# Gate products on VectorE, quartered group loads and a later first stage in a fused FFT and MLP kernel with gradients (one Trainium2 core)

## The chip, the cores and the metric

The kernel runs on one NeuronCore of one Trainium2 chip. A core has five engines that run their own instruction queues: TensorE (PE in the profile, with its weight loads as PEld), VectorE (DVE), ScalarE (ACT), GpSimd (POOL) and SyncE (SP). In this kernel SP issues the loads and POOL issues the stores and a few small loads. The metric is the device time of one launch in microseconds, as the median of several runs.

## The reference, cut to what matters

The reference runs a forward function and its gradients for eight inputs. S is 2048, D is 1024, F is 3584, and all data is bf16.

```python
g = sigmoid((x * gate_w).sum(-1, keepdims=True))
a = irfft2(rfft2(x) * (w_r + 1j * w_i))           # over S and D
h = relu(x @ w1 + b1);  b = (h * h) @ w2 + b2
out = g * a + (1 - g) * b
# B_x is not used in either branch; the outputs are out and the gradients
# of A_x, A_w_r, A_w_i, B_w1, B_b1, B_w2, B_b2, gate_w
```

Both branches and the gate read the same x, A_x in the call. The gate needs one dot product of 1024 elements for each of the 2048 rows.

## The kernel before, in words

The rows of x and of the incoming gradient are cut into 16 tiles of 128 rows (NT = 16). The kernel is written in a language in which tiles come from pools with a tag and a number of buffers. The waits between engines are derived from what each instruction reads and writes, and the order of each engine's queue is planned at build time, from the order of the code (as a priority) and from when inputs are thought to be ready. `after(ins, earlier)` (L210) adds a dependency by hand: a real wait, or, with `NoSync`, only an order. The order of the work is otherwise set by Python generators: each `yield` ends a step, and `spread` (L948) takes a given number of steps of a side generator for every step of a main one.

**MLP in (L635).** `mlp_in` makes the hidden layer and its gradient, transposed. `hidden` (L644) is eight matmuls of 512 columns into a PSUM tile `ph` (L647); ACT writes `rT` (L649) and its square `h2T` (L650). `grads` (L653) is eight matmuls into `pd` (L657), and DVE writes `dhT` (L661). `ph` and `pd` share one tag with two buffers. Both need transposed inputs: `xT` from x, and `dbT` from `dbn`, the incoming gradient scaled by 1 - g. `turn_tile` (L571) makes these with eight TensorE transposes of 128 columns into a PSUM tile `pt`, copied out by ACT for x (`turn_x`) and by DVE for the gradient (`turn_grad`). `pt`, the gate's `pg` and other small PSUM tiles share a tag `tr` with two buffers.

**The gate (L584).** For a group of four row tiles, `gate` runs 32 matmuls with one output column each (L590): a block of xT is the stationary operand and a column of `gwcol` (gate_w turned into columns by `vectors`, L578) the moving one. ACT makes the two sigmoids `omg` = 1 - g and `gcol` = g (L594, L595), and DVE scales four tiles of dbn in place by omg (L597).

**The start (L976 to L1029).** Seven matmuls on zeros warm TensorE up. Then, by hand: four tiles of x are loaded, turned and gated, and a loop over k = 0 to 3 interleaves eight units of `mlp_in` (four hidden, four grads) with the turning of four gradient tiles, and with the loads, turning and gating of the next four x tiles. The first stage of the FFT of x (`first_stage_of_x`, L599, with `folds` on DVE, `row_stage` L244 and `first_columns` L256 on TensorE) starts at the end of k = 0. After the loop 72 further units are mixed with the rest of this stage and with the same stage of the gradient, 0.9 steps a unit (L1036).

**Weight gradients and the middle of the FFT (L743, L415, L473).** `mlp_grads` runs 14 jobs: seven groups of 512 hidden columns of h2 against dbn (L786, gradient of w2) and seven of dh against x (L802, gradient of w1). A job is eight units of 16 matmuls of 512 columns; after each unit ACT copies the result to `wo` (L790, L807), and POOL stores it. The operand `grp` of a job is a group of h2 or dh that is read back from DRAM and turned by the DMA (`group`, L749, through `turned`, L166): four loads of 512 KB, in a tile with two buffers. They are written at the start of the job before the one that uses them. `spread` (L1054) mixes `fft_mid` and half of `fft_out` into the jobs, so that the SP queue also carries their loads z, w, amat, apmat and r. In `fft_out`, `folded` (DVE, L495) and `rows_back` (L503) use a loaded tile r, `columns_back` (L282 by `column_stage`) gives `pui`, ACT copies it to `e` (L512, L513), DVE makes `yo` (L529), and POOL stores it to `ax_scr` (L532).

**MLP out (L827).** The last stage makes the output (L872) and the gradient of x (L932), with the rest of `fft_out`. The change doesn't touch it. The multiply-and-sum operation that the change uses for the gate is already used there (L850, on f32 and bf16).

Of the kernel before, what the change touches and what calls it, by code (L numbers as in the profile page):

```python
# [10 lines left out]
P = 128  # L11
# [114 lines left out]
def kernel(  # L126
# [63 lines left out]
    kf = pers.tile([P, P], FDT, name="kf", tag="kf")  # L190
    cols = lambda n, w, dt=FP32: pers.tile([P] + w, dt, name=n, tag=n)
    gcol, omg, gpg, aGo, dsc = (cols(n, [NT]) for n in ("gcol", "omg", "gpg", "aGo", "dsc"))
    gwcol = cols("gwcol", [DC], BF16)
    bGo = cols("bGo", [NT, NH])
    gb1part = cols("gb1part", [FC, g.NSB])
    b1col = cols("b1col", [FC])
# [276 lines left out]
    def fft_out():  # L473
# [62 lines left out]
                    ld(out=w2[:, fc : fc + 4, :], in_=B_w2[fc * P : (fc + 4) * P, :].rearrange("(q p) e -> p q e", p=P))  # L536

        load(0), load(1)
        folded(0)
        for n in range(len(tiles) + 1):  # L540
            if n < len(tiles):
                rows_back(n)
                yield
            if n > 0:
                columns_back(n - 1)
            if n + 2 < len(tiles):
                load(n + 2)
            if n + 1 < len(tiles):
                folded(n + 1)
            yield  # L550
# [24 lines left out]
            nc.tensor.transpose(pt[:, b, :], src[:, b * P : (b + 1) * P], identb[:])  # L575
        copy(out=dst[:, :, of_tile(i)], in_=pt[:])

    def vectors(vrow):  # L578
        vps = tps.tile([P, FC + DC], BF16, name="vps", tag="tr", bufs=2)
        nc.tensor.transpose(vps[:], vrow[:], identb[: FC + DC, : FC + DC])  # L580
        nc.vector.tensor_copy(out=b1col[:], in_=vps[:, 0:FC])
        nc.vector.tensor_copy(out=gwcol[:], in_=vps[:, FC : FC + DC])

    def gate(i0):  # L584

        c_ = slice(i0, i0 + 4)
        pg = tps.tile([P, 4], FP32, name="pg", tag="tr", bufs=2)
        for i in range(i0, i0 + 4):
            for dc in range(DC):
                mm(  # L590
                    pg[:, i - i0 : i - i0 + 1], lhsT=xT[:, dc, of_tile(i)], rhs=gwcol[:, dc : dc + 1],
                    start=(dc == 0), stop=(dc == DC - 1), skip_group_check=True,
                )
        nc.scalar.activation(omg[:, c_], pg[:], ACT.Sigmoid, scale=-1.0)  # L594
        nc.scalar.activation(gcol[:, c_], pg[:], ACT.Sigmoid)  # L595
        for i in range(i0, i0 + 4):
            nc.vector.tensor_scalar(out=dbn[:, i, :], in0=dbn[:, i, :], scalar1=omg[:, i : i + 1], scalar2=None, op0=ALU.mult)  # L597

# [144 lines left out]
    def mlp_grads():  # L743
# [2 lines left out]
        strm = later["strm"]  # L746
        acc = wb.tile([P, D], FP32, name="dbacc", tag="dbacc")

        def group(scr, fg, earlier=None):  # L749
            t_ = strm.tile([P, NT, FGW], BF16, name="grp", tag="strm", bufs=2)  # L750
            v_ = scr[:].rearrange("c p s -> (c p) s")[fg * FGW : (fg + 1) * FGW, :]
            for k in range(4):
                after(turned(t_[:, 4 * k : 4 * (k + 1), :], v_[:, 4 * k * P : 4 * (k + 1) * P]), earlier)
            return t_

        xr = []
        jobs = [(h2T_scr, fg) for fg in range(FG)] + [(dhT_scr, fg) for fg in range(FG)]
        nxt = group(*jobs[0], later["blocks"])
        nc.vector.tensor_copy(out=acc[:], in_=dbn[:, 0, :])
        for t in range(1, NT):  # L760
            V(out=acc[:], in0=acc[:], in1=dbn[:, t, :], op=ALU.add)
        for n, (scr, fg) in enumerate(jobs):
            cur = nxt
            if n + 1 == len(jobs):
                later["block"] = blocks(h2T_scr)(0)
            else:
                nxt = group(*jobs[n + 1], later["blocks"])
            if n == 1:
                column_sums(wb, tps, "tr", acc, out_7)

# [9 lines left out]
            if scr is h2T_scr:  # L780
                for fb_ in range(FGC):
                    wo = wb.tile([P, D], BF16, name="wo2", tag="wo2", bufs=2)
                    for hf in range(NH):
                        pw = mps.tile([P, H], FP32, name="pw", tag="pw", bufs=2)
                        for t in range(NT):
                            mm(  # L786
                                pw[:], lhsT=cur[:, t, fb_ * P : (fb_ + 1) * P], rhs=dbn[:, t, hf * H : (hf + 1) * H],
                                start=(t == 0), stop=(t == NT - 1),
                            )
                        last = nc.scalar.copy(out=wo[:, hf * H : (hf + 1) * H], in_=pw[:])  # L790
                        if n in (2, 3):
                            x_ = wb.tile([P, D], BF16, name=f"res1_{len(xr)}", tag=f"res1_{len(xr)}")
                            after(ld(out=x_[:], in_=x_perm[len(xr)]), last)
                            xr.append(x_)
                        yield 3
                    f0 = fg * FGW + fb_ * P
                    st(out=out_6[f0 : f0 + P, :], in_=wo[:])
            else:
                for d_ in range(DC):
                    pw = mps.tile([P, FGW], FP32, name="pw", tag="pw", bufs=2)  # L800
                    for t in range(NT):
                        mm(  # L802
                            pw[:], lhsT=xr[t][:, d_ * P : (d_ + 1) * P], rhs=cur[:, t, :],
                            start=(t == 0), stop=(t == NT - 1),
                        )
                    wo = wb.tile([P, FGW], BF16, name="wo1", tag="wo1", bufs=3)
                    nc.scalar.copy(out=wo[:], in_=pw[:])  # L807
                    st(out=out_4[d_ * P : (d_ + 1) * P, fg * FGW : (fg + 1) * FGW], in_=wo[:])
                    yield 3
        mpss.close()  # L810
# [162 lines left out]
        turn_tile(dbT, i, dbn[:, i, :], nc.vector.tensor_copy)  # L973


    zeros = f1.tile([P, H], BF16, name="zeros", tag="zeros")  # L976
    nc.vector.memset(zeros[:], 0.0)
    pz = tps.tile([P, H], FP32, name="pz", tag="tr", bufs=2)
    for _ in range(7):
        mm(pz[:], lhsT=zeros[:, 0:P], rhs=zeros[:], start=True, stop=True)  # L980

    units = mlp_in()
    rows_of_x(0)
    vrow = f1.tile([FC + DC, P], BF16, name="vrow", tag="vrow")
    st(out=vrow[0:FC, :], in_=B_b1.rearrange("(fc p) -> fc p", p=P))
    st(out=vrow[FC : FC + DC, :], in_=gate_w.rearrange("(fc p) -> fc p", p=P))
    next(units)
    rows_of_grad(0)
    st(out=kf[:], in_=cten["kf"].ap())
    for i in range(4):  # L990
        turn_x(i)
    vectors(vrow)
    gate(0)
    next(units)
    rows_of_x(1)
# [2 lines left out]
    for k in range(NT // 4):  # L998
# [1 line left out]
        if k + 1 < NT // 4:  # L1000
            rows_of_grad(k + 1)
        next(units)
        turn_grad(i), turn_grad(i + 1)
        next(units)
        turn_grad(i + 2)
        next(units)
        turn_grad(i + 3)
        next(units)
        if stage:
            next(stage)  # L1010
        next(units)
        if k + 1 < NT // 4:
            turn_x(i + 4), turn_x(i + 5)
        next(units)
        if k + 1 < NT // 4:
            turn_x(i + 6), turn_x(i + 7)
        next(units)
        if k + 1 < NT // 4:
            gate(4 * (k + 1))
        if k + 2 < NT // 4:  # L1020
            rows_of_x(k + 2)
        if k == 0:
            for n in range(3):
                xs[n] = source(n, x_perm)
            stage = first_stage_of_x()
        next(stage)
        next(units)
        next(stage)
    V(out=gpg[:], in0=gcol[:], in1=omg[:], op=ALU.mult)  # L1029
    def firsts():  # L1030
        yield from stage
# [1 line left out]

    first = firsts()
    n = 0
    mixed = spread(units, first, 0.9)  # L1036
    while n < 72:
        next(mixed)
        n += 1
# [10 lines left out]

    spec, grads = spectra(), mlp_grads()
    next(grads), next(grads)
    todo = 1 + 12 * (S2 // 2) + 2 * NT
    for _ in spread(grads, spec, todo / (2.0 * FG * FGC * NH - 2)):  # L1054
        pass
    tps_s.close()
# [38 lines left out]
```

## Time and profile before

| | |
|---|---|
| time, median of 3 runs | 1309.12 us (1309.04 to 1311.78) |
| profiled span | 1308.4 us |
| ACT busy | 424.5 us (32%) |
| DMA: turned loads of groups, h2 and dh | 28 and 28 issues, 5.7 and 6.0 us to landing (median) |
| TensorE's granted clock | 1.000 |

The span is the time from the first to the last instruction in the profile. In a line of a timeline the columns are the start and the duration in us, the engine, the line of the code, the operation, output <- inputs, shapes and count; the brackets hold the idle time of the engine just before it and what ended that. In the line of a wait the columns are who waited for whom, the total in us, the number of times and the longest. SPq is the queue of SP: it holds DMA issues, and a merged line gives the time from the first to the last issue. PE's matmuls overlap, so one of 512 columns is shown with 379 ns while the next starts some 216 ns after it.

### The profile page before, as it was taken

What the parts mean: (1) busy time and instruction counts of PE and PEld (TensorE: products, weight loads), DVE (VectorE), ACT (ScalarE), POOL (GpSimd) and SP (SyncE); (2) the same over time, 40 slices, a digit from 0 to 9 for tenths busy, and PEclk for the clock granted to TensorE, in tenths of its full rate; (3) what the DMA queues carried; (4) which work ended last, traced back from release to release, by engine and by line L of the source; (5) the groups of instructions that cost most, each with busy time, mean ns of one, the idle gap of its engine ahead of it and who ended that gap; (6) DMA issues with size and microseconds to landing.
All of it is one profiled execution on the core that took longest, in us unless ns stands there. A gap on an engine that the chain in (4) does not pass through costs nothing. (4 is left out here: it accounts for less than half of the span.)

```text
span 1308.4 us, 18055 instructions
## 1 busy us (share of the span) xinstructions
PE 1289.1 (99%) x6922; PEld 627.4 (48%) x7057; DVE 682.6 (52%) x1516; ACT 424.5 (32%) x722; POOL 191.3 (15%) x337
## 2 busy tenths in 40 slices
PE   8999999999999999999999999999999999999998
PEld 5555544555544444444444445554444444444443
DVE  3554424444312495677766772445767678722222
ACT  5656655666533323323233333342111111000000
POOL 0111111111110122122113221221000001000000
PEclk9999999999999999999999999999999999999999
DMA  9566354554526688898797759956999986743440
GB/s 298 181 185 178 129 155 144 184 142 157 146 97 161 173 217 183 240 242 197 185 178 159 156 140 272 306 193 175 224 198 216 228 202 195 215 130 105 131 119 25
DMA packets 314280, 234.20 MB, mean 179 GB/s; under 512 B 183701, under 2 KB 263601, under 8 KB 314193
## 3 DMA queue, kind: packets, MB, share of 16 engines
q1 hardware_dynamic: 289552, 150.58, 48.7%
q0 software_dynamic: 24640, 82.46, 19.0%
q8 instruction: 55, 0.90, 0.3%
q14 instruction: 33, 0.26, 0.1%
HBM read 107.14 MB, written 81.81 MB: 144 GB/s over the span
## 5 line engine op out<-in xcount | busy, mean ns | idle before, releaser
L647 PE MATMUL ph<-xT,w1g 128*128 128x512 bf16 x862 | 217.0, 379 | 1.7
L657 PE MATMUL pd<-dbT,w2T 128*128 128x512 bf16 x879 | 209.9, 379 | 1.1
L802 PE MATMUL pw<-grp,res 128*128 128x512 bf16 x872 | 200.0, 379 | 1.9 <-ACT wo L807 0.7
L786 PE MATMUL pw<-dbn,grp 128*128 128x512 bf16 x875 | 199.6, 379 | 1.1
L872 PE MATMUL acc<-w,hblk 128*128 128x512 bf16 x875 | 195.7, 379 | 1.1
L661 DVE SCALAR_TENSOR_TENSOR dhT<-pd,rT 128x512 bf16<-128x512 f32 x112 | 77.4, 691 | 228.6 <-PE pd L657 170.2
L932 PE MATMUL accg<-w1Tr,hblk 128*128 128x512 bf16 x878 | 192.9, 379 | 0.9
L932 PEld LDWEIGHTS <-hblk 128*128 128x128 bf16 x896 | 87.4, 98 | 105.7 <-issue 0.9
L657 PEld LDWEIGHTS <-w2T 128*128 128x128 bf16 x896 | 87.2, 98 | 102.5
L786 PEld LDWEIGHTS <-grp 128*128 128x128 bf16 x896 | 86.8, 98 | 103.2 <-issue 0.9
L872 PEld LDWEIGHTS <-hblk 128*128 128x128 bf16 x896 | 86.3, 98 | 98.5
L802 PEld LDWEIGHTS <-res 128*128 128x128 bf16 x896 | 86.2, 98 | 98.6 <-issue 1.0
L647 PEld LDWEIGHTS <-w1g 128*128 128x128 bf16 x896 | 84.7, 98 | 89.1
L649 ACT ACTIVATE rT<-ph,b1col 128x512 bf16<-128x512 f32 x112 | 76.9, 686 | 111.2 <-PE ph L647 107.9
L936 DVE TENSOR_TENSOR gxo<-accg,g 128x512 bf16<-128x512 f32 x32 | 22.1, 690 | 120.9 <-PE accg L932 120.9
L790 ACT CAST wo<-pw 128x512 bf16<-128x512 f32 x56 | 32.7, 584 | 142.1 <-PE pw L786 136.0
L807 ACT CAST wo<-pw 128x512 bf16<-128x512 f32 x56 | 32.8, 585 | 136.6 <-PE pw L802 78.4
L650 ACT ACTIVATE h2T<-rT 128x512 bf16<-128x512 bf16 x112 | 70.5, 629 | 2.5
L505 ACT CAST rt<-pki 128x1024 f16<-128x1024 f32 x32 | 32.6, 1018 | 98.1 <-PE pki L503 98.0
L331 DVE TENSOR_TENSOR x<-px,common 128x1024 f16<-128x1024 f32 x32 | 38.8, 1220 | 40.7 <-ACT common L328 40.7
L532 POOL DMA_DIRECT2D ax_scr<-yo x32 | 17.3, 540 | 235.4 <-DVE yo L531 223.9
L873 DVE SCALAR_TENSOR_TENSOR ot<-acc,omg,af 128x512 bf16<-128x512 f32 x32 | 23.9, 747 | 52.8 <-PE acc L872 52.7
(182 smaller groups left out, 1300.8 us busy)
## 6 DMA issues: line engine op xcount, KB each, us to landing
h2T_scr<-h2T POOLq DMA_DIRECT2D x28, 512.0 KB, 4.2
dhT_scr<-dhT POOLq DMA_DIRECT2D x28, 512.0 KB, 4.9
hblk<-h2T_scr SPq DMA_DIRECT2D x8, 1792.0 KB, 8.6
hblk<-dhT_scr SPq DMA_DIRECT2D x8, 1792.0 KB, 8.5
z_scr<-u POOLq DMA_DIRECT2D x32, 256.0 KB, 2.9
z<-z_scr SPq DMA_DIRECT2D x16, 512.0 KB, 4.9
y_scr<-pc POOLq DMA_DIRECT2D x16, 512.0 KB, 7.5
r<-y_scr SPq DMA_DIRECT2D x32, 256.0 KB, 3.8
```

Source lines behind the costliest of these rows:

```text
L331: V(out=x[:, j, :, 0:H].rearrange("p c (i g) -> p c i g", g=4), in0=px[:].rearrange("p c (g i) -> p c i g", g=4), in1=common[:].rearrange( ...
L647: mm(ph[:], lhsT=w1g[:, dc, fc % 2 * P : (fc % 2 + 1) * P], rhs=xT[:, dc, ss], start=(dc == 0), stop=(dc == DC - 1))
L649: nc.scalar.activation(rT[:], ph[:], ACT.Relu, bias=b1col[:, fc : fc + 1])
L650: nc.scalar.activation(h2T, rT[:], ACT.Square)
L657: mm(pd[:], lhsT=w_[:, ec, fc % FGC * P : (fc % FGC + 1) * P], rhs=dbT[:, ec, ss], start=(ec == 0), stop=(ec == DC - 1),)
L661: return STT(out=dhT, in0=pd[:], scalar=2.0, in1=rT[:], op0=ALU.mult, op1=ALU.mult, accum_out=gb1part[:, fc, sb : sb + 1],)
L786: mm(pw[:], lhsT=cur[:, t, fb_ * P : (fb_ + 1) * P], rhs=dbn[:, t, hf * H : (hf + 1) * H], start=(t == 0), stop=(t == NT - 1),)
L790: last = nc.scalar.copy(out=wo[:, hf * H : (hf + 1) * H], in_=pw[:])
L802: mm(pw[:], lhsT=xr[t][:, d_ * P : (d_ + 1) * P], rhs=cur[:, t, :], start=(t == 0), stop=(t == NT - 1),)
L807: nc.scalar.copy(out=wo[:], in_=pw[:])
L872: turn["PE"] = mm(acc[:], lhsT=cur[:, fc, t2 * P : (t2 + 1) * P], rhs=w2[:, fc, cs], start=(fc == 0), stop=(fc == FC - 1))
L932: turn["PE"] = mm(acc[:], lhsT=cur[:, fc, t2 * P : (t2 + 1) * P], rhs=w1T[:, fc, cs], start=(fc == 0), stop=(fc == FC - 1),)
```

## The change

The change has five parts.

1. **The gate by dot products.** The gate's matmuls, gwcol and pg go. gate_w is broadcast to all partitions (`gw_bc`), and DVE makes the dot product of each row tile with it in one multiply-and-sum (`gate_dot`), which reads the loaded tile of x rather than xT. It is meant to free TensorE.
2. **The table first.** One sigmoid on a zero stands ahead of the program, so that ACT's function table for sigmoid is loaded at the start rather than at the first gate. The warm-up is now 25 matmuls of 128 columns, on a smaller block of zeros.
3. **Order in the first loop.** The turns of gradient tiles move by one unit, for k = 0 more than for the others.
4. **The first stage of x** starts at the end of k = 1 rather than k = 0, a step in the middle of each k goes, and the mixing rate after the loop is 0.95 rather than 0.9.
5. **Quarters.** For jobs 1 to 12 the four turned loads of the next group are no longer written together at the job's start. Each waits for ACT's copy of one unit (0, 1, 3 and 4 of the eight), so that other transfers can go between them. `fft_out` has three empty steps more at its start, counted in `todo`.

```diff
-    gwcol = cols("gwcol", [DC], BF16)
+    gdot = cols("gdot", [NT])
...
         load(0), load(1)
+        yield
+        yield
         folded(0)
+        yield
...
+    def gate_dot(i):
+        junk = f1.tile([P, D], BF16, name="junk", tag="zeros")
+        nc.vector.tensor_tensor_reduce(
+            out=junk[:], in0=rows[i][:], in1=gw_bc[:], scale=1.0, scalar=0.0,
+            op0=ALU.mult, op1=ALU.add, accum_out=gdot[:, i : i + 1],
+        )
...
     def gate(i0):
         c_ = slice(i0, i0 + 4)
-        pg = tps.tile([P, 4], FP32, name="pg", tag="tr", bufs=2)
-        for i in range(i0, i0 + 4):
-            for dc in range(DC):
-                mm(
-                    pg[:, i - i0 : i - i0 + 1], lhsT=xT[:, dc, of_tile(i)], rhs=gwcol[:, dc : dc + 1],
-                    start=(dc == 0), stop=(dc == DC - 1), skip_group_check=True,
-                )
-        nc.scalar.activation(omg[:, c_], pg[:], ACT.Sigmoid, scale=-1.0)
-        nc.scalar.activation(gcol[:, c_], pg[:], ACT.Sigmoid)
+        nc.scalar.activation(omg[:, c_], gdot[:, c_], ACT.Sigmoid, scale=-1.0)
+        nc.scalar.activation(gcol[:, c_], gdot[:, c_], ACT.Sigmoid)
...
-        def group(scr, fg, earlier=None):
+        def group(scr, fg):
             t_ = strm.tile([P, NT, FGW], BF16, name="grp", tag="strm", bufs=2)
             v_ = scr[:].rearrange("c p s -> (c p) s")[fg * FGW : (fg + 1) * FGW, :]
-            for k in range(4):
+            def quarter(k, earlier):
                 after(turned(t_[:, 4 * k : 4 * (k + 1), :], v_[:, 4 * k * P : 4 * (k + 1) * P]), earlier)
-            return t_
+            return t_, quarter
...
-                nxt = group(*jobs[n + 1], later["blocks"])
+                nxt, quarter = group(*jobs[n + 1])
+                if n == 0:
+                    for k in range(4):
+                        quarter(k, later["blocks"])
+            quarters = {0: 0, 1: 1, 3: 2, 4: 3} if 0 < n < len(jobs) - 1 else {}
...
                         last = nc.scalar.copy(out=wo[:, hf * H : (hf + 1) * H], in_=pw[:])
+                        if 2 * fb_ + hf in quarters:
+                            quarter(quarters[2 * fb_ + hf], last)
...
-                    nc.scalar.copy(out=wo[:], in_=pw[:])
+                    last = nc.scalar.copy(out=wo[:], in_=pw[:])
+                    if d_ in quarters:
+                        quarter(quarters[d_], last)
...
-    nc.vector.memset(zeros[:], 0.0)
+    nc.vector.memset(zeros[:, 0:P], 0.0)
+    nc.scalar.activation(gdot[:, 0:1], zeros[:, 0:1], ACT.Sigmoid)
     pz = tps.tile([P, H], FP32, name="pz", tag="tr", bufs=2)
-    for _ in range(7):
-        mm(pz[:], lhsT=zeros[:, 0:P], rhs=zeros[:], start=True, stop=True)
+    for _ in range(25):
+        mm(pz[:, 0:P], lhsT=zeros[:, 0:P], rhs=zeros[:, 0:P], start=True, stop=True)
...
-    st(out=vrow[FC : FC + DC, :], in_=gate_w.rearrange("(fc p) -> fc p", p=P))
+    gw_bc = f1.tile([P, D], BF16, name="gw_bc", tag="gw_bc")
+    st(out=gw_bc[:], in_=gate_w.partition_broadcast(P))
...
     for i in range(4):
+        gate_dot(i)
         turn_x(i)
-    vectors(vrow)
+    vectors()
...
         next(units)
-        turn_grad(i), turn_grad(i + 1)
+        if k > 0:
+            turn_grad(i)
         next(units)
-        turn_grad(i + 2)
+        turn_grad(i + 1) if k > 0 else turn_grad(i)
         next(units)
+        turn_grad(i + 2) if k > 0 else (turn_grad(i + 1), turn_grad(i + 2))
         turn_grad(i + 3)
         next(units)
-        if stage:
-            next(stage)
         next(units)
         if k + 1 < NT // 4:
-            turn_x(i + 4), turn_x(i + 5)
+            gate_dot(i + 4), turn_x(i + 4), gate_dot(i + 5), turn_x(i + 5)
         next(units)
         if k + 1 < NT // 4:
-            turn_x(i + 6), turn_x(i + 7)
+            gate_dot(i + 6), turn_x(i + 6), gate_dot(i + 7), turn_x(i + 7)
...
-        if k == 0:
+        if k == 1:
...
-    mixed = spread(units, first, 0.9)
+    mixed = spread(units, first, 0.95)
...
-    todo = 1 + 12 * (S2 // 2) + 2 * NT
+    todo = 4 + 12 * (S2 // 2) + 2 * NT
```

## The prediction

> **What bounds the kernel now.** I read the page first, then the waits of PE, then PE's timeline around each wait, then the DVE and DMA-issue timelines there. The page's first part:
>
> ```profile
> PE 1289.1 (99%) x6922; PEld 627.4 (48%) x7057; DVE 682.6 (52%) x1516; ACT 424.5 (32%) x722; POOL 191.3 (15%) x337
> ```
>
> TensorE (PE) is busy 1289.1 of 1308.4 us, and its clock row is at the top in every slice. So an edit is worth what it takes out of PE's queue, or out of PE's 19.3 us of idle time. Some 4 us of that are the end of the program (PE stops at 1304.6 in the chain), and some 6 us are gaps of 0.05 us at every 10.8 us, which no edit touches. The waits of PE name the rest:
>
> ```profile
> PE pui L282 <- ACT e L513: 2.3, 1, 2.3
> PE pt L575 <- DMA identb<-c_identb: 1.3, 1, 1.3
> ...
> PE pw L802 <- ACT wo L807: 0.7, 1, 0.7
> PE vps L580 <- ACT xT L576: 0.6, 1, 0.6
> PE pk L249 <- ACT f L241: 0.5, 2, 0.3
> ```
>
> The two large ones outside the start (columns: total, times, longest) are one event. The timeline of all engines there:
>
> ```profile
> 845.79 0.43 DVE L529 TENSOR_TENSOR yo<-tt 128x512 f16<-128x512 f16 x1 [1.67 <-DMA ax_scr<-yo]
> 846.99 3.61 PE L802 MATMUL pw<-grp,res 128*128 128x512 bf16 x16 [0.66 <-ACT wo L807]
> 851.77 0.58 ACT L807 CAST wo<-pw 128x512 bf16<-128x512 f32 x1 [3.92 <-DMA out_dram<-wo]
> 852.69 0.42 DVE L495 TENSOR_TENSOR rf<-r 128x256 f16<-128x256 f16 x1 [6.05 <-DMA r<-y_scr]
> 853.38 0.68 PE L282 MATMUL pui<-ci,rt 128*128 128x256 f16 x8 [2.34 <-ACT e L513]
> ```
>
> DVE and ACT wait for DMA (yo and wo stores to leave their buffers, r to arrive), and PE behind them. What filled the DMA is in the issue queue:
>
> ```profile
> 822.74 5.61 SPq L488 DMA_DIRECT2D r<-y_scr  x2
> 830.09 15.79 SPq L166 DMA_TRANSPOSE grp<-dhT_scr  x4
> 845.99 12.10 SPq L488 DMA_DIRECT2D r<-y_scr  x4
> ```
>
> Four turned loads of a group go out back to back for 15.8 us, and no r between them. Last, the gate and the start, on PE's timeline:
>
> ```profile
> 10.47 0.95 PE L590 MATMUL pg<-gwcol,xT 128*128 128x1 bf16 x32 [0.35 <-DVE gwcol L582]
> ...
> 26.94 0.94 PE L590 MATMUL pg<-gwcol,xT 128*128 128x1 bf16 x32
> 27.75 1.89 PE L657 MATMUL pd<-dbT,w2T 128*128 128x512 bf16 x8
> ```
>
> Each later gate holds PE from 26.94 to 27.75.
>
> [...] the multiply-and-sum of L850 (f32 by bf16) takes 1219. [...] the trace has 681 to 691 ns for such adds of 1024. [...] the trace has 1.28 us at 10.83. [...] here the first transposes at 5.72 take 1.86 us for 16, later ones 1.06.
>
> **The change, part by part.**
>
> *Gate matmuls.* 128 matmuls and weight loads leave PE. Three gates in the loop, 0.81, 0.80 and 0.80 us by start-to-start: −2.4 us. At the start, xT's fourth copy ends at 10.81 and the first hidden matmul starts at 11.50, the gate standing between; it can now start near 10.9: −0.6 us.
>
> *Table first.* The second load at 10.83 delays the sigmoids to 12.12, but PE worked on hidden matmuls until the first turn of dbn at 13.01 with no idle time. Nothing on PE's path; hidden before, and gone after.
>
> *Dots on DVE.* 16 multiply-and-sums of 1024 bf16 by bf16. Bounds: 0.69 us (the bf16 add) and 1.22 us (L850), each with an accumulator read of 0.08. I take 1.2 us from start to start, since ops overlap by some 0.08: 19 us of DVE within the first 70, where DVE is busy under two thirds. Where does this reach PE? Each ph and pd shares two PSUM banks, so DVE must empty a pd before the second matmul group after it.
>
> First four dots: they wait for the broadcast of gate_w. It stands third in POOL's queue (issue near 2.5 us); kf and cf beside it took 5.7 and 6.8 us to land, so it lands near 8.5. Dots end near 13.5, sigmoids and b1col near 14, rT of the first hidden near 14.7. PE's third hidden starts about 10.9 + 2×1.73 + 0.45 = 14.8 and needs that bank: just hidden. Behind the fourth dot queue b1col and the dbn scales; turn_grad comes a unit later for that, and costs nothing there. But turns 1, 2 and 3 of k = 0 now follow each other: the third needs the first's pt, with a copy of 0.69 and 0.2 of signalling against 0.45 of transposing: +0.4 us.
>
> Dots of the next x tiles, k = 0: x loads are issued at 17.21 (behind w2T's turned loads, 10.2 us), and PE turned the first at 21.70. From pd0 to the point where PE needs pd3's bank, PE has 4×1.73 + 2×0.89 = 8.7 us. DVE has four pd (4×0.77 = 3.1), four dots (4.8) and four dbn scales (1.67, timeline at 28.13): 9.6, and 0.2 of signalling. So PE waits about 1.1 us. For k = 1 and 2 the x tiles are there long before (DVE idle 3.2 us before 41.38), and dots can run in that hole: 0.2 us each. Sum: +1.5 us.
>
> *Shorter warm-up, 25 matmuls of 128 columns:* it ends before identb arrives at 5.72, which releases the transposes as before: nothing. *First stage of x one k later, 0.95 for 0.9:* the same PE work moved. Of 73 steps 6 instead of 11 go into the loop, and 67/0.95 = 70.5 of 72 units hold the rest: nothing. It takes 2.3 us folds out of DVE's k = 0, which the dots fill. The two pk waits (0.5 us) I expect again one k later.
>
> *Quarters.* Group n+1 for n = 1 to 12 now goes out in four parts behind units 0, 1, 3 and 4. L786 starts at 444.8 and L802 ends at 897: 452/14 = 32.3 us a job, 4.04 a unit. Each part waits on SP for its unit's ACT copy; behind it on SP queue z, w, r and res loads, issued at most a unit later than now, with two or three buffers. In return they and the stores meet one turned load (median issue 3.05 us for dhT) at a time rather than four. The 3.0 us event at 846 to 853 goes: −3.0. The three waits of 0.2 us (pvs, pv) I leave. Does the last part arrive? Issued 20.2 us into the job, its rows are wanted after 3×4.04 + 12×0.216 = 14.7 us; issue and landing (median 5.8) take 8.9: hidden. *Three yields and todo + 3:* no PE work; the first L503 shows no wait before, so nothing.
>
> Sum: −2.4 −0.6 −3.0 +0.4 +1.5 = −4.1 us: 1309.1 becomes **1305.0**.
>
> **Rivals.**
>
> *DVE blocked for a load (0.24): 1309.* DVE takes its queue in order, and the order is planned at build time: gpg, written behind the whole loop, stands at 69.31 before a pd of it, so ready work is pulled ahead. If the planner thinks the x tiles of k = 0 come earlier than they do, dots stand ahead of the dbT copies. A copy then waits for a load landing near 21.5 and a dot or two, and pd starts near 25 where it could at 19.4. That eats 5.5 of −6.0 + 0.4: about 0. For it: rf blocked DVE for r 8 times, 36.4 us. Against: if the plan has PE and the loads right, the copies stand first.
>
> *Quarters late (0.12): 1312, slower.* The longest landing is 13.2 us; with an issue of 3.05 that is 16.2 against 14.7, 1.5 late, and an SP wait ahead adds to it. A mean of 0.6 us at each of 12 boundaries gives +7. For it: DMA is 0.84 to 0.96 busy in the stretches from 470 to 602. Against: a quarter alone competes with fewer turned loads.
>
> *All hidden (0.12): 1303.* Dots at 0.8 us or well placed: DVE's 9.6 becomes 8.0 and the waits vanish: −6.0.
>
> **How the numbers follow.** The forecast has 0.52, spread by 1.5 us each way. Faster means under 1306.5, slower over 1311.7. Forecast: 0.47 faster, 0.05 same. All hidden: 0.12 faster. Blocked: 0.05, 0.11, 0.08. Late quarters: 0.12 slower. Sum: 0.64, 0.16, 0.20. The range goes from 1302 (all hidden and no pk wait) to 1311.5, leaving out a tenth above, and little below.
>
> **What would show it.** In the profile after: no L590; one ACT_TABLE_LOAD; first ph near 10.9; dots at 1.2 us; PE waits for dhT of 1 to 2 us in all before 80 us; no PE wait over 1 us between 800 and 897; turned loads of a group spaced 4 to 8 us apart on SP. The prediction is wrong if a dot waits for an x tile with a dbT copy behind it, if PE waits for grp at the jobs' starts, or if PE is still at half rate in its first hidden matmuls.

## The result, and the profile after

| | before | after |
|---|---|---|
| time, median (range), 4 runs each on one chip | 1310.16 us (1309.04 to 1311.78) | 1324.97 us (1322.45 to 1325.91) |
| ratio to before, 95% interval | | 1.0109 (1.0089 to 1.0129) |
| profiled span | 1308.4 us | 1324.1 us |
| TensorE's granted clock, mean | 1.000 | 0.994 |

The change makes the kernel about 1.1% slower. The first part of the page, the engines' busy time:

```profile
PE 1290.9 (97%) x6812; PEld 627.1 (47%) x6947; DVE 704.1 (53%) x1547; ACT 424.5 (32%) x722; POOL 193.9 (15%) x337
```

PE's busy time hardly moved, but it now goes with 15.7 us more of span: the loss is idle time of PE, and matmuls at a lower clock, which count as busy (from 848 to 850 us, below, the clock is 0.50 and PE is busy 2.00 of 2.00 us). Where it went is read from the first matmul of each stage. In these answers by tile (after), the figures behind the colon are the shortest, median and longest duration in ns, then the first and last start:

```profile
L649 PE MATMUL ph<-xT,w1g x868: 376/379/634, 11.9 to 445.7; 128*128 128x512 bf16 x174
L797 PE MATMUL pw<-dbn,grp x875: 376/379/389, 447.6 to 674.8; 128*128 128x512 bf16 x175
L815 PE MATMUL pw<-grp,res x872: 376/379/634, 675.7 to 910.6; 128*128 128x512 bf16 x175
L887 PE MATMUL acc<-w,hblk x875: 377/379/634, 911.8 to 1123.6; 128*128 128x512 bf16 x175
L947 PE MATMUL accg<-w1Tr,hblk x877: 377/379/390, 1124.5 to 1319.9; 128*128 128x512 bf16 x176
```

| stage | begins before | begins after | longer by |
|---|---|---|---|
| start and MLP in | 0 | 0 | 2.6 us |
| jobs of h2 | 445.0 | 447.6 | 2.2 us |
| jobs of dh | 670.9 | 675.7 | 9.3 us |
| MLP out, L887 | 897.7 | 911.8 | 2.3 us |
| gradient of x, L947 | 1108.1 | 1124.5 | −0.7 us |

The sum is the 15.7 us. A longest matmul of 634 ns instead of some 380 marks a stage in which PE ran slowly for a time. The waits of PE name the rest:

```profile
PE pw L815 <- DMA grp<-dhT_scr: 9.4, 2, 8.6
PE pv L378 <- DVE y L453: 1.8, 7, 0.6
PE pt L578 <- DMA xsrc<-in_A_x_dram: 1.6, 3, 0.9
PE ph L649 <- DVE dhT L663: 1.5, 2, 0.8
PE ph L649 <- DMA w1g<-in_B_w_dram: 1.5, 1, 1.5
PE pd L659 <- DVE dbT L579: 1.5, 1, 1.5
```

None of these but pv was in the list before. The 3.0 us of pui and wo are gone, as meant; in their place, PE waits 9.4 us for the quarters of a group. (Of the 2.2 us that the jobs of h2 are longer by, 1.2 are four of the waits of pv for y; the rest was not traced.) At the group, the timeline of PE:

```profile
835.30 1.89 PE L815 MATMUL pw<-grp,res 128*128 128x512 bf16 x8
838.06 1.02 PE L815 MATMUL pw<-grp,res 128*128 128x512 bf16 x4 [0.87 <-DMA grp<-dhT_scr]
847.65 1.87 PE L815 MATMUL pw<-grp,res 128*128 128x512 bf16 x4 [8.57 <-DMA grp<-dhT_scr]
```

The first unit of the job stops before its last eight matmuls: it gets the third quarter 0.87 us late and the fourth 8.57 us late. SP's queue says why:

```profile
801.13 1.53 SPq L536 DMA_DIRECT2D w<-in_B_w_dram  x2
807.33 9.62 SPq L166 DMA_TRANSPOSE grp<-dhT_scr  x1
817.06 0.51 SPq L488 DMA_DIRECT2D r<-y_scr  x1
817.62 0.42 SPq L536 DMA_DIRECT2D w<-in_B_w_dram  x1
818.14 7.33 SPq L166 DMA_TRANSPOSE grp<-dhT_scr  x1
825.52 0.57 SPq L536 DMA_DIRECT2D w<-in_B_w_dram  x1
826.19 0.44 SPq L488 DMA_DIRECT2D r<-y_scr  x1
826.69 0.42 SPq L536 DMA_DIRECT2D w<-in_B_w_dram  x1
827.21 8.81 SPq L166 DMA_TRANSPOSE grp<-dhT_scr  x1
836.12 0.52 SPq L488 DMA_DIRECT2D r<-y_scr  x1
836.73 4.11 SPq L166 DMA_TRANSPOSE grp<-dhT_scr  x1
```

Issuing the four quarters held SP for 9.62, 7.33, 8.81 and 4.11 us, 29.9 us in all, in a job of 32.3. The last one was issued at 836.73, when its own job had been running since 835.30, and it landed 10.9 us later. Between them go the loads of w2 for the last stage (L536 in `fft_out`, 1 MB each). After the wait the granted clock is low as well. Windows of all engines (the last three figures are PE's clock, the DMA's share and GB/s):

```profile
844.00:848.00 4.00, 0.34 (x1) 0.10 (x1) 0.00 (x0) 0.00 (x0) 0.00 (x0) 0.50 1.05 291
848.00:850.00 2.00, 2.00 (x10) 1.07 (x9) 0.76 (x2) 0.40 (x1) 0.00 (x0) 0.50 0.22 83
```

The start, on the timeline of all engines:

```profile
9.94 1.23 DVE L588 CUSTOM_DVE_ANT_0 junk<-xsrc,gw_bc 128x1024 bf16<-128x1024 bf16 x1 [8.98 <-DMA gw_bc<-in_gate_w_dram]
11.87 0.61 PE L649 MATMUL ph<-xT,w1g 128*128 128x512 bf16 x1 [1.49 <-DMA w1g<-in_B_w_dram]
12.70 4.45 PE L649 MATMUL ph<-xT,w1g 128*128 128x512 bf16 x14 [0.22 <-issue]
16.99 0.61 PE L578 MATMUL pt<-identb,dbn 128*128 128x128 bf16 x8
...
22.70 1.23 DVE L588 CUSTOM_DVE_ANT_0 junk<-xsrc,gw_bc 128x1024 bf16<-128x1024 bf16 x1 [1.60 <-DMA xsrc<-in_A_x_dram]
...
23.86 0.69 DVE L579 COPY dbT<-pt 128x1024 bf16<-128x1024 bf16 x1
...
24.69 1.89 PE L659 MATMUL pd<-dbT,w2T 128*128 128x512 bf16 x8 [1.45 <-DVE dbT L579]
...
48.15 1.23 DVE L588 CUSTOM_DVE_ANT_0 junk<-xsrc,gw_bc 128x1024 bf16<-128x1024 bf16 x1 [1.25 <-DMA xsrc<-in_A_x_dram]
51.32 1.90 PE L649 MATMUL ph<-xT,w1g 128*128 128x512 bf16 x8 [0.81 <-DVE dhT L663]
```

A dot of 1.23 us stands on DVE ahead of the copy of dbT, and itself waits 1.60 us for a tile of x; PE waits behind both. At 48.15, in k = 1, it is the same again: a dot waits for a tile of x, a second dot follows, and dhT comes behind them; PE waits 0.81 us and, at 54.41, another 0.69. The first 16 hidden matmuls take 5.12 us (11.87 to 16.99) where 16 at 0.216 us would take 3.46. The stage's account: first hidden 0.37 later than before, +1.66 at the low rate, +1.45 for dbT, +1.5 for dhT, −2.4 for the gates that are gone: +2.6, which is what the table shows. It is the account of one execution. In seven profiles of kernels that keep the start of the kernel before, the first recorded hidden matmul begins anywhere from 9.76 to 11.50 us, and the first eight take up to 3.26 us (quarters_alone) instead of 1.73, so the first two items are no sure mark of the change. The end of the stage is: the jobs of h2 begin between 444.0 and 446.0 in these seven, and between 447.6 and 449.7 in the four profiles with parts 1 to 4 whole.

### The profile page after: what moved, and what is told of

It reads as the page before. It is cut to its first block, busy times and chain, and to the rows that moved or that the text cites. A ratio compares the mean times of both kernels' runs of the same rounds, so it can differ in the third digit from the quotient of the medians.

```text
span 1324.1 us, 17889 instructions
## 1 busy us (share of the span) xinstructions
PE 1290.9 (97%) x6812; PEld 627.1 (47%) x6947; DVE 704.1 (53%) x1547; ACT 424.5 (32%) x722; POOL 193.9 (15%) x337
## 4 chain that ended last, share of the span: by engine, by line
PE 76%; issue 11%; DMA 4%; DVE 4%; POOL 3%; ACT 1%; SPq 1%; POOLq 0%; DVEq 0%; ACTq 0%
PE pd L659 15%; PE accg L947 15%; PE ph L649 14%; PE acc L887 13%; PE pw L797 7%; PE pw L815 5%; DMA z<-z_scr 2%; DMA out_dram<-wo 1%; PE pu L282 1%; POOL out_dram L823 1%; PE pk L249 1%; PE pt L578 1%; DMA w1g<-in_B_w_dram 1%; PE pui L282 1%; DMA b_bc<-in_B_b_dram 1%
## 5 line engine op out<-in xcount | busy, mean ns | idle before, releaser
L649 PE MATMUL ph<-xT,w1g 128*128 128x512 bf16 x868 | 219.8, 381 | 4.5 <-DVE dhT L663 1.5
L815 PE MATMUL pw<-grp,res 128*128 128x512 bf16 x872 | 201.4, 380 | 10.9 <-DMA grp<-dhT_scr 9.4
L887 PE MATMUL acc<-w,hblk 128*128 128x512 bf16 x875 | 197.5, 381 | 1.1
L947 PE MATMUL accg<-w1Tr,hblk 128*128 128x512 bf16 x877 | 192.7, 379 | 1.0
L947 PEld LDWEIGHTS <-hblk 128*128 128x128 bf16 x896 | 87.5, 98 | 105.9 <-issue 0.9
L887 PEld LDWEIGHTS <-hblk 128*128 128x128 bf16 x896 | 86.7, 98 | 99.7 <-issue 2.3
L512 ACT CAST e<-pui 128x512 f16<-128x512 f32 x32 | 18.8, 587 | 105.2 <-PE pui L282 85.1
L888 DVE SCALAR_TENSOR_TENSOR ot<-acc,omg,af 128x512 bf16<-128x512 f32 x32 | 24.0, 749 | 46.6 <-PE acc L887 46.5
```

Of the source, the lines that this page charges most:

```text
L649: mm(ph[:], lhsT=w1g[:, dc, fc % 2 * P : (fc % 2 + 1) * P], rhs=xT[:, dc, ss], start=(dc == 0), stop=(dc == DC - 1))
L815: mm(pw[:], lhsT=xr[t][:, d_ * P : (d_ + 1) * P], rhs=cur[:, t, :], start=(t == 0), stop=(t == NT - 1),)
L887: turn["PE"] = mm(acc[:], lhsT=cur[:, fc, t2 * P : (t2 + 1) * P], rhs=w2[:, fc, cs], start=(fc == 0), stop=(fc == FC - 1))
L947: turn["PE"] = mm(acc[:], lhsT=cur[:, fc, t2 * P : (t2 + 1) * P], rhs=w1T[:, fc, cs], start=(fc == 0), stop=(fc == FC - 1),)
```

## The experiments

All ratios are to the kernel before, run beside it on the same chip, with 95% intervals. Chips differ between experiments (the kernel before beside them has medians from 1309.54 to 1311.82 us), so times from different ones are compared by their ratios; a profile shows one execution. Two groups ask what the start costs and what the quarters cost; a third puts mends together.

**start_alone** is the change without part 5: parts 1 to 4 on the kernel before.

> The changed kernel with the group loads and the empty steps of fft_out as before: parts 1 to 4 of the change alone. Theory A (two separate losses: a slow start, and late quarters): the job stage begins near 447.6 us as in the changed kernel (445.0 before), and the rest is as before, so 1309 + 3 = about 1312 to 1313 us. Theory B (the quarters are the whole loss, and the start gains as predicted): about 1306 us. Theory C (the order of later stages is disturbed by any change at the start): over 1318 us.

Measured: 1314.74 us, ratio 1.0040 (1.0028 to 1.0051), before 1309.87. The jobs of h2 begin at 448.4. First hidden at 12.52 after 2.43 us of waiting for w1g; 16 hidden in 5.71 us; dbT 1.45 and dhT 1.5. So parts 1 to 4 are by themselves a loss of some 5 us, and the waits in this stage are those of the whole change. (The event at 846 to 853 is here too: PE waits 1.96 us for wo.)

**broadcast_alone** is the kernel before with the new load, whose result nothing reads:

```diff
+    gw_bc = f1.tile([P, D], BF16, name="gw_bc", tag="gw_bc")
+    st(out=gw_bc[:], in_=gate_w.partition_broadcast(P))
```

> The kernel before with the broadcast load of gate_w added at the start and read by nothing. Theory D: the hidden matmuls wait for w1g and start 1 to 2 us later, many of the first 16 at half rate: 1309.9 + 2 to 3 us. Theory E: within 0.5 us of the kernel before.

Measured: 1312.88 us, 1.0021 (1.0011 to 1.0031), before 1310.11. PE's timeline:

```profile
12.10 3.19 PE L647 MATMUL ph<-xT,w1g 128*128 128x512 bf16 x7 [1.98 <-DMA w1g<-in_B_w_dram]
```

The load alone brings back the wait for w1g, and some 2.8 us of loss. It brings 256 KB, one row of 2 KB 128 times. Between 6 and 8 us all DMA together moved 336 GB/s before, 265 with this load, 195 in the change; the first two loads of w1g landed in 7.3 us before, in 9.2 and 9.0 with it (median of the two). The slow first matmuls come with it here, but quarters_alone has them without this load.

**row_by_pe** is start_alone with the row loaded once and spread over the partitions by two matmuls with ones:

```diff
-    st(out=gw_bc[:], in_=gate_w.partition_broadcast(P))
+    st(out=gw_row[0:1, :], in_=gate_w.rearrange("(o d) -> o d", o=1))
...
+        mm(pgw[:], lhsT=ones_r[0:1, :], rhs=gw_row[0:1, hf * H : (hf + 1) * H], start=True, stop=True)
+        nc.vector.tensor_copy(out=gw_bc[:, hf * H : (hf + 1) * H], in_=pgw[:])
```

> Parts 1 to 4 of the change (start_alone), but gate_w is loaded as one row of 2 KB and spread over the partitions by two TensorE matmuls against ones, instead of a DMA that reads that row 128 times. Theory D (the broadcast load holds the DMA engines and delays x and w1g): x tiles 2 and 3 and w1g land as early as in the kernel before, no wait for w1g, hidden starts by 11.5 us and runs at full rate; 3 to 4 us less than start_alone (1314.7), about 1311. Theory E (the first loads are late for another reason, such as the order in the queues): within 1 us of start_alone.

Measured: 1314.17 us, 1.0032 (1.0014 to 1.0050), before 1310.11. The wait for w1g is gone (landing 7.4 us), but the two matmuls stand in PE's queue and wait 2.98 us for the row, with the transposes behind them; the first hidden matmul comes at 13.34. The gain of 3 to 4 us that was expected is not there. One wait for another: a test of the cause, not a mend.

**after_warm7** is the change with the old warm-up of seven matmuls of 512 columns.

> The changed kernel with seven warm-up matmuls of 512 columns in place of 25 of 128. In the changed kernel the first two hidden groups (16 matmuls from 11.87 us) run at half rate. If the shorter warm-up is the cause, they run at full rate here and the time falls by about 1.7 us (1322 to 1323). If the thin PE work from 5 to 12 us is the cause (waits for x and w1g), they are at half rate here too and the time stays within 0.5 us.

Measured: 1320.69 us, 1.0089 (1.0054 to 1.0123), before 1309.87. The first 16 transposes take 1.32 us from 4.51 instead of 1.86, yet the first 16 hidden matmuls still take 5.31 us, behind 2.84 us of waiting for w1g. So the shorter warm-up is not what makes them slow; in the whole time the two can't be told apart (1.0089 against 1.0109, with overlapping intervals).

**first_by_pe** is start_alone with the first four tiles gated on TensorE as before, and the broadcast held until the first rT; the later dots stay where the change put them.

```diff
-        gate_dot(i)
         turn_x(i)
...
+        if k == 0:
+            after(st(out=gw_bc[:], in_=gate_w.partition_broadcast(P)), later["rT"])
```

> Parts 1 to 4 (start_alone, 1314.7 us), but the first four tiles are gated on TensorE as before, and the broadcast of gate_w is held until rT of the first hidden group; the dots of the other three groups stay where the change has them, one of them ahead of the last dbT copy of k = 0. If the broadcast and the first dots made most of the start's loss: no w1g wait, first hidden at full rate, and only the waits for dbT and dhT (about 3 us) against 2.4 us of gates saved: 1310 to 1311. If the place of the later dots made it: 1313 to 1315.

Measured: 1310.43 us, 1.0003 (0.9991 to 1.0015), before 1310.07. No wait for w1g; dbT still 1.33 and dhT 2.2 us. The first 16 hidden matmuls still take 5.22 us, with no wait directly ahead of them, so that the wait for w1g is not what makes them slow. The ratio is 0.0037 lower than start_alone's, some 4.8 us: most of the start's loss is the early broadcast and the first four dots behind it, which go together here; broadcast_alone puts 2.8 us on the load by itself.

**late_dots** goes further: only the last two groups of four are gated by dots, in the hidden halves of k = 1 and 2 and in DVE's order behind the last dhT; the broadcast waits for the first dhT. Table, warm-up and turns are as before (no parts 2 and 3); the first stage of x starts a k later and is mixed at 0.95, as in part 4.

```diff
+        if i0 < 8:
+            pg = tps.tile([P, 4], FP32, name="pg", tag="tr", bufs=2)
...
+        else:
+            pg = gdot[:, c_]
...
+        dots = [i + 4, i + 5, i + 6, i + 7] if k in (1, 2) else []
```

> The kernel before with the dots of groups 2 and 3 (tiles 8 to 15) on DVE, written into the hidden halves of k = 1 and 2, groups 0 and 1 on TensorE as before, the broadcast of gate_w held until the first pd is out (about 22 us), and the first stage of x one k later with 0.95. Theory J (what cost time in part 1 was the place, the broadcast at the start and dots ahead of pd and dbT, not DVE's load): 2 gates of 0.8 us go and no new wait over 0.5 us comes: 1310.1 - 1.6 = 1308.5. Theory K (DVE has no room for dots within the first 60 us at all): waits of 1.5 us or more for dhT or dbT, 1310 to 1312.

Measured: 1309.49 us, 0.9988 (0.9973 to 1.0003), before 1309.54. No wait for dbT or dhT, and the jobs of h2 begin at 442.8 instead of 445.0. Two gates of 0.8 us off PE, and dots that stand ahead of nothing: 2.2 us gained in that stage. The same start in best and best_wo3 (below) gives 442.7 twice, against 444.0 to 446.0 in the seven profiles with the old one. In the whole time of late_dots nothing of it is seen: the interval holds 1.

Now the quarters. **quarters_alone** is the kernel before with the quarters but not the empty steps; **quarters_yields** has both, all of part 5.

> The kernel before with the group loads in quarters, and nothing else. Theory A: PE waits for grp of dh between 800 and 860 us for 6 to 10 us, about 1316 to 1320 us in all. Theory B: the whole loss and more, about 1325 us. If the late group came from the shift by the empty steps, no wait for grp and 1306 to 1309 us.

> The kernel before with the quarters and the three empty steps of fft_out (part 5 whole). Theory A: the changed kernel less its loss at the start, about 1322 us less 3 = 1319 to 1322 us, with a wait for grp of 8 to 9 us and PE at half rate after it. If the empty steps matter little: the same as quarters_alone within 2 us.

Measured: quarters_alone 1312.71 us, 1.0021 (1.0012 to 1.0031); quarters_yields 1317.97 us, 1.0060 (1.0042 to 1.0077); before 1309.87 for both. PE's timeline of the first:

```profile
795.97 0.41 PE L503 MATMUL pki<-ki,r 128*128 128x128 f16 x4 [3.01 <-DMA r<-y_scr]
```

and of the second:

```profile
838.99 1.87 PE L816 MATMUL pw<-grp,res 128*128 128x512 bf16 x4 [3.40 <-DMA grp<-dhT_scr]
```

Either way the event at 846 to 853 us is gone and another wait has its place: without the empty steps PE comes to `rows_back` before r is there; with them, r is in time but the quarters are late, and PE waits for y (at pv, 1.6 us in seven waits, 0.2 without the steps) and rf (2.1 us) too. The quarters alone lose 2.8 us, and no group is late, where 6 to 10 us of waiting were expected; the empty steps, which were to cost nothing, add 5. A group is late only with both; the steps without the quarters were not tried. Part 5 whole loses 8 us, parts 1 to 4 lose 5; together 13 of the 14.8.

**quarters_early** gives the quarters to units 0, 1, 2 and 3 in place of 0, 1, 3 and 4, in quarters_yields.

> Part 5 on the kernel before, with the quarters behind units 0, 1, 2 and 3 rather than 0, 1, 3 and 4. Theory G: the last quarter is issued a unit (4 us) earlier, so the wait for grp of 3.4 us goes: about 1312 to 1314 us. Theory F: SP's queue is already late there, so its issue moves by less than 2 us and a wait of 1.5 to 3 us stays: 1316 to 1318 us.

Measured: 1320.12 us, 1.0079 (1.0056 to 1.0103), before 1310.11. The group wait falls to 0.5 us, but a result store in the jobs of h2 is now late (pw for wo, 2.9 us) and r is late again (1.9 us). In this profile one late transfer is exchanged for others.

**w2_paced** is quarters_yields with each w2 load held until ACT's copy of the tile it is written beside:

```diff
-            nc.scalar.copy(
+            half = nc.scalar.copy(
...
-                    ld(out=w2[:, fc : fc + 4, :], in_=B_w2[fc * P : (fc + 4) * P, :].rearrange("(q p) e -> p q e", p=P))
+                    after(ld(out=w2[:, fc : fc + 4, :], in_=B_w2[fc * P : (fc + 4) * P, :].rearrange("(q p) e -> p q e", p=P)), half)
```

> Part 5 on the kernel before (quarters_yields, 1318.0 us), with each of the seven loads of w2 (1 MB) held until ACT's copy of its own tile in fft_out. Theory F (the late quarters come from the collision with w2, of which seven went out within 28 us): no wait for grp, 3.4 us and the half rate after it go, about 1312 to 1314 us. Theory G (the fourth quarter is issued too late whatever else runs): the wait for grp stays over 2 us and the time is within 1.5 us of quarters_yields.

Measured: 1309.00 us, 0.9992 (0.9982 to 1.0001), before 1310.11. No wait for a group is left, and the ratio is 0.0068 below quarters_yields, some 9 us; 4 to 6 were expected, and 2 of the 9 come without the quarters as well (before_w2_paced, below). Nothing of the quarters was changed: what made this group late were the w2 loads, which are free to go as soon as SP comes to them. In the change seven went out within 28 us (798.6 to 826.7), among the quarters.

**w2_paced_no_yields** takes the empty steps out of w2_paced.

> w2_paced (1309.0 us) without the three empty steps of fft_out and with todo as before, so quarters and paced w2 loads alone. If the empty steps are needed against the wait for r at the start of fft_out (3.0 us in quarters_alone at 796 us): that wait stays, and the time is 1 to 2 us over w2_paced, since the waits of pv for y (1.3 us) and the waits for rf after 897 us (1.1 us) go. If they only do harm: 1 to 3 us under w2_paced.

Measured: 1312.04 us, 1.0017 (1.0005 to 1.0028), before 1309.54. r is 3.92 us late at 797. With quarters and the w2 loads held, the empty steps are worth about 3 us (0.0025 of the ratio); with these loads free, they cost 5.

**before_w2_paced** is the kernel before, whole group loads and all, with only the w2 loads held.

> The kernel before with only the pacing of the seven w2 loads (each held until ACT's copy of its own tile in fft_out). Theory H (the w2 loads, not the four turned loads together, made the 3.0 us event at 846 us): PE's waits for wo and e between 800 and 897 us go, 1310.1 - 3 = about 1307. Theory I (the four turned loads back to back made it): the event stays within 1 us, 1309 to 1310.

Measured: 1307.34 us, 0.9983 (0.9975 to 0.9991), before 1309.54. The largest wait left outside the start, from PE's timeline:

```profile
755.25 0.39 PE L326 MATMUL pxs<-sums,amat 128*128 128x512 f16 x1 [1.56 <-DVE sums L319]
```

The event at 846 to 853 us, which the quarters were to remove, is gone without them, with the four turned loads still together, and the 2.2 us gained are near the 3 expected of theory H. So holding the w2 loads is enough. That they alone made the event is not shown: the profiles of first_by_pe and late_dots, with whole groups and w2 free, have no wait of PE there either, though a store is late:

```profile
844.43 0.59 ACT L820 CAST wo<-pw 128x512 bf16<-128x512 f32 x1 [4.61 <-DMA out_dram<-wo]
```

That is late_dots. With w2 held ACT still waits 4.30 us for a store, at 828.37. ACT's wait of 3.92 us for a store in the profile before went with 2.34 us of waiting for PE, these of 4.61 and 4.30 us with none there, and one profile without the event proves little; the time of 22 runs proves more.

**after_w2_paced** is the whole change with the w2 loads held; **after_both** has also the start of first_by_pe.

> The changed kernel with the w2 loads paced. If the two losses add up: no wait for grp, and the 9 us that the pacing took off part 5 on the kernel before come off here too: 1325.0 - 9 = 1316, which is start_alone (1314.7) within 2 us. If the late group in the changed kernel has another cause: a wait for grp of 3 us or more stays and the time is over 1319.

> The changed kernel with both: w2 loads paced, first four tiles gated on TensorE, broadcast held. If the three causes found (broadcast, w2 collision, dots ahead of dbT and dhT) are all that is wrong: 1309.5 to 1311.5, within 0.2% of the kernel before. If something else in the change costs time: 1313 or more.

Measured, before 1310.07: after_w2_paced 1313.18 us, 1.0026 (1.0018 to 1.0035); after_both 1317.95 us, 1.0061 (1.0041 to 1.0081). The first mend takes some 11 us off the change. The second, which was worth 4.8 us without part 5, makes it worse by about as much. PE's timeline of after_both:

```profile
9.70 0.95 PE L603 MATMUL pg<-gwcol,xT 128*128 128x1 bf16 x32 [0.35 <-DVE gwcol L586]
21.62 0.62 PE L579 MATMUL pt<-identb,xsrc 128*128 128x128 bf16 x8 [2.20 <-DMA xsrc<-in_A_x_dram]
23.73 3.57 PE L671 MATMUL pd<-dbT,w2T 128*128 128x512 bf16 x8 [1.49 <-DVE dbT L580]
...
517.99 3.61 PE L809 MATMUL pw<-dbn,grp 128*128 128x512 bf16 x16 [2.19 <-ACT wo L813]
```

PE gets through its first hidden matmuls sooner and then stands for 2.20 us before the next tile of x. That tile's load is issued at 17.99, behind the turned loads of w2T which hold SP for 11.21 us, whatever PE does. After this wait and the one for dbT, eight matmuls take 3.57 us instead of 1.89. At 518 a result buffer of the jobs of h2 comes free late; the matmuls behind it run at the full rate (16 in 3.45 us), not slower as the next expectation has it.

**after_both_wo3** and **best_wo3** (best is below) give these result tiles three buffers:

```diff
-                    wo = wb.tile([P, D], BF16, name="wo2", tag="wo2", bufs=2)
+                    wo = wb.tile([P, D], BF16, name="wo2", tag="wo2", bufs=3)
```

> The changed kernel with both mends and a third buffer for the result tiles of the jobs of h2. Theory that a late store costs the rest: in the kernel with both mends one store of 256 KB of a result tile, issued at 507.9 us, let its buffer go only at 517.4, so that TensorE waited 2.2 us and then ran 16 matmuls in 6.5 us in place of 6.1, some of them at half rate. With a third buffer no wait for a result tile is left in the jobs of h2, their stage falls from 231.0 to about 227 us, and the time from 1317.95 to 1311 to 1314 us. Rival, that the two mends don't add for another reason: the wait goes and the time stays above 1316 us.

> The best kernel (gate dots later in the first stage, w2 loads held) with a third buffer for the result tiles of the jobs of h2. Its profile shows no wait for a result tile. Theory: the late store happens in some executions only, so the third buffer takes at most 1 us off the median: 1305 to 1307 us. Rival: nothing at all, or a loss of up to 2 us because the results leave later together: 1306 to 1309 us.

Measured, before 1311.82: after_both_wo3 1317.71 us, 1.0049 (1.0036 to 1.0063). The wait for wo is gone and the stage is 228.5 us long instead of 231.0, yet the time stays: the x tile is 1.90 us late again, and at 681 to 684 PE waits 2.78 and 1.97 us for quarters of the first group of dh, which no w2 load is near. So the late store was not the missing part. The late x tile is in both kernels; late quarters are only in the second's profile. How the 6 to 8 us divide is not settled.

**best** is late_dots with the w2 loads held: the gate's dots where DVE is free, no quarters, no empty steps.

> late_dots and before_w2_paced together: with theories H and J 1310.1 - 1.6 - 3 = about 1305.5; with I and J 1308.5; with H and K 1307 to 1309.

Measured: 1306.38 us, 0.9979 (0.9967 to 0.9992), before 1309.54; best_wo3 1305.81 us, 0.9960 (0.9947 to 0.9973), before 1311.82. Both are faster than the kernel before and the changed one. They were measured on different chips and their intervals overlap, so what the third buffer adds is not told apart.

## Why the prediction was wrong

The prediction said 1305.0 us, faster, with a range to 1311.5; it is 1325.0. Its mechanisms were mostly in the list, two of them as rivals with small chances, and both came true together. All three signs that it named for being wrong came, the third as slow matmuls. Of its sum, parts 1 to 4 were to give −1.1 us (−2.4, −0.6, +0.4, +1.5) and cost 4.9 (start_alone); part 5 was to give −3.0 and cost 8.1 (quarters_yields).

- **Quarters (−3.0): failed, and the largest error.** The event at 846 to 853 did go. The step that failed is "issue and landing (median 5.8) take 8.9: hidden". It took the median issue of 3.05 us for a place where the DMA is full (share 1.10 and 288 GB/s from 807 to 841 us, 0.80 and 202 from 445 to 1108, in the profile after): there the four issues took 29.9 us rather than 12.2, and the landing 10.9 rather than 5.8. The fourth was to be issued some 12 us before its job began and was issued 1.4 us after. The rival "Quarters late" named this, but put it down as 1.5 us at worst plus a mean of 0.6 a boundary, +7 in all. Measured: at 12 boundaries one wait, of 9.4 us, in one place, with half-rate matmuls behind it (clock 0.50 from 848 to 850). Under it lies a narrow reading of the event: the four turned loads back to back were taken for what filled the DMA. before_w2_paced keeps them and has no event. The loads of w2, in the same queue, which the prediction does not mention, are the ones whose holding pays. A whole group written at its job's start had 32.3 us to absorb them; quarters had given that slack away. The quarters by themselves exchange the event for a wait for r (quarters_alone, +2.8 us); a group was late only with the empty steps as well.
- **Three yields (0): failed.** They add no work to PE, but they shift the mixing, and with the quarters they cost 5 us (quarters_yields against quarters_alone). They save r's wait of 3 to 4 us, and they bring the late group, six or seven waits of pv for y (1.3 to 1.8 us) and waits for rf (0.8 to 2.1 us). The kernels without them have a single wait of pv for y of 0.2 to 0.4 us.
- **Dots on DVE (+1.9): a dot right in size, their order wrong.** A dot takes 1.22 us as taken from L850 (1.27 from start to start, for 1.2). PE waits 1.5 us for dhT, the sum predicted, but that is luck: 1.1 of it was to come in k = 0, and none does; all of it comes from k = 1, where the x tiles were to be "there long before" and a dot waits 1.25 us for one. The +0.4 for the turns does not show. What failed is the order: "if the plan has PE and the loads right, the copies stand first". They do not; a dot that waits for x stands ahead of the dbT copy, 1.45 us. The rival "DVE blocked for a load" is this, mis-sized: 1.45 us, not 5.5. That the broadcast "lands near 8.5" was a little early (the first dot starts at 9.94), and what it does to other loads was not costed at all.
- **Gate matmuls (−2.4, and −0.6 at the start): half right.** late_dots shows the gain where nothing stands in the way: two gates gone, 2.2 us in that stage, though it moves the first stage of x as well and the whole time doesn't show it. The −0.6 failed: PE was ready for its first hidden matmul, and w1g was not, because of the broadcast (broadcast_alone). In the profile it turned into +0.4, and 1.7 us of slow matmuls whose cause is open.
- **Shorter warm-up (0):** nothing speaks against it; after_warm7, with the old one, is not told apart. **Table first (0):** one table load is left (1.28 us at 0.73, where the kernel before had two of 1.28 us, at 0.72 and 10.83), and PE waits nowhere for a sigmoid; not tried alone. **First stage one k later (0):** nothing speaks against it, and late_dots has it; not tried alone.

The remaining loss: +2.3 us in MLP out, where PE waits 1.24 and 0.78 us for rf at 932 and then runs at half rate (clock 0.50 from 934 to 936). It goes with the empty steps: quarters_yields has 2.1 us of rf, w2_paced 1.1 us, the kernels without the steps 0.2 at most.

## What to carry to other kernels

A transfer that lands in time with a median issue and landing may be late where the queue is full (here four issues took 29.9 us rather than 12.2), so cost it in the stretch where it will run, and ask which transfers in that stretch are not needed yet: here holding those back gained 2.2 us, and cutting up the one that was in sight lost 2.8. Before work is moved to an engine with spare time, look at what stands behind it in that engine's queue (here the dbT copy, 1.45 us of waiting for PE), and at what its new operand does to the loads around it (here the landing of w1g, 9.2 us instead of 7.3). And a gain at the start of a chain ends at the next input that comes by its own clock, as the x tiles did here (2.20 us of waiting in after_both).

## What the runs showed of the hardware that was not expected

- A load that reads one row of 2 KB for 128 partitions slows the loads beside it: 265 instead of 336 GB/s between 6 and 8 us, and the landing of w1g from 7.3 to 9.2 us (7.4 in row_by_pe, where the row is loaded once, 2 KB). A plain load of 256 KB in its place was not tried.
- The issue of a turned load of 512 KB on SP took 2.4 us at the median in the jobs of dh after the change and up to 9.6 us among the 1 MB loads of w2; what is behind it on SP goes out after it (one was issued from 807.33 for 9.62 us, the next load at 817.06). In the jobs of h2, with no such load, one took 8.0 us, so what makes an issue long is not settled.
- A low clock came behind two short waits of PE close together. After 1.24 and 0.78 us of waiting, with one matmul of 0.23 us between them, it was 0.50. In quarters_yields, after 1.29 and 0.78 us, the next 28 matmuls of L888 took 7.66 us instead of 6.20; in after_warm7, after 0.88 and 0.77 at the same place, 28 took 6.21. What sets the clock is not shown by these runs. Windows of the profile after, the clock being the third figure from the end:

```profile
928.00:932.00 4.00, 2.87 (x17) 1.31 (x14) 3.96 (x12) 0.00 (x0) 0.54 (x1) 1.00 1.21 298
932.00:934.00 2.00, 1.11 (x7) 0.54 (x8) 1.97 (x9) 0.45 (x1) 0.00 (x0) 0.86 1.29 191
934.00:936.00 2.00, 2.00 (x6) 0.75 (x5) 1.97 (x6) 0.56 (x1) 0.54 (x1) 0.50 1.20 333
```

Six matmuls in 2 us at the last. In late_dots the first eight hidden matmuls took 2.92 us from start to start instead of 1.73, with no wait over 0.35 us in the 5 us ahead of them, so what makes them slow at the start stays open. In the change it isn't even settled that it is the clock: the windows from 12 to 16 us, with 13 matmuls in 4 us, show a granted clock of 1.00.
